# Folding the next batch at the end of the first layer in place of beside the second layer

## The chip, the cores and the metric

The kernel runs on one core of one Trainium2 chip. The metric is device time in microseconds (us) from the first to the last instruction. Engines are named as the profile names them: PE is the matrix engine (PEld its weight loads), DVE the vector engine, ACT the scalar engine, POOL the GpSimd engine and SP the engine whose queue issues most transfers. PSUM is the memory into which PE writes its sums; it is divided into banks, and here each bank tile holds 128 x 512 floats. L927 means line 927 of the kernel's source.

## The reference

There are 8 batches of 576 tokens. An attention with 8 heads gives each token a row of 512 numbers. Then follow a Fourier transform over tokens and columns, of which the real part is added, a normalisation of each row, and two matrix products with a ReLU between them.

```python
q_s = softmax(q, axis=-1); k_s = softmax(k, axis=2)          # cut: written out in full
kv = np.einsum('bhsd,bhse->bhde', k_s, v)                    # one 64x64 matrix per head
x  = np.einsum('bhsd,bhde->bhse', q_s, kv)                   # then heads side by side: (8, 576, 512)
mixed = np.real(np.fft.fft(np.fft.fft(x, axis=1), axis=2))
u  = x + mixed
un = (u - mean(u)) / sqrt(var(u) + 1e-06)
out = u + np.maximum(un @ w_ch1, 0) @ w_ch2                  # 512 -> 2048 -> 512
```

Everything is float32.

## The kernel before

The main loop works on groups of 512 tokens. While PE does the two layers of one group, the vector engines and PE prepare the next batch. For each group `up` is the first layer, `down` is the second. `front(b)` gives two lists of side steps for batch b: `one` is the attention, `two` is the transform and the mixing. The function `merged` spreads a side list evenly over a main list.

```python
def mixed(main, side):
    steps = []
    for i, step in enumerate(main):
        steps.append(step)
        steps += side[i * len(side) // len(main):(i + 1) * len(side) // len(main)]
    return steps
# ... cut
for order, g in enumerate(groups):                # groups 0..6, then 8, then 7
    one, two = front(order + 1, loads) if order + 1 < B else (blk.later, [])
    # ... cut: group 0 has its own, plain form
    jobs, down = blk.up(order, nexts.pop(g)), blk.down(g, order)
    merged(flat(jobs), one)
    merged(down, two + (norm(groups[order + 1]) if order < B else []))
```

From group 1 on, both layers use a Strassen scheme with seven products instead of eight. A first layer is four jobs. Each job runs its products in the order 1, 6, 5, 7, 2, 4, 3 in only three PSUM banks, `ba`, `bb` and `bc`, with one buffer each. Product 7 is added onto product 6 in bank `bb`, so `bb` must have been read (L927) before product 7 may start.

```python
def m1():
    nc.scalar.copy(temp("s1"), box["ba"][:])                                    # L923, ACT
def m6():
    V.tensor_tensor(out=temp("u2"), in0=box["bb"][:], in1=box["s1"][:], op=ALU.add)   # L927, DVE
def m7():
    V.tensor_tensor(out=temp("u3"), in0=box["bb"][:], in1=box["s1"][:], op=ALU.add)   # L931, DVE
    # ... cut
at = {1: "ba", 2: "ba", 6: "bb", 7: "bb", 4: "bb", 5: "bc", 3: "bc"}            # ORDER = (1, 6, 5, 7, 2, 4, 3)
```

In `up` the matmuls are L959. The sums of the last three products go to SBUF on DVE (L970), through the ReLU on ACT (L971), and are then combined on POOL (L363 to L366). In `down` the matmuls are L997; a product is four times as long as in `up`.

The end of the attention of a batch, and the four fold steps with which its transform begins:

```python
def t_times_kv(self, b):                                  # last step of `one`
    # ... PE L672 -> px; ACT copies it to g (L675); PE L678 -> a second px; ACT L679
    V.scalar_tensor_tensor(out=g[:, 1:HD], ...)           # L680, DVE
    V.tensor_tensor(...); V.tensor_tensor(...)            # L682, L683, DVE

def tokens_folded(some=range(4)):                         # two on POOL, two on DVE
    e.tensor_tensor(out=eo[i][:, 0:D], in0=x[i % 2, 0], in1=x[i % 2, 1], op=op)            # L701
def columns_folded(some=range(4)):                        # two on POOL, two on DVE
    e.tensor_tensor(out=t[:, 1:HD], in0=t[:, 1:HD], in1=t[:, D - 1:HD:-1], op=op)          # L707
def by_frequency(some=range(4)):                          # two on POOL, two on DVE
    e.tensor_tensor(out=eo[i][:, NN:], in0=one[:, 0:NN], in1=two[:, 0:NN], op=op)          # L716
def columns_again(some=(2, 3, 0, 1)):                     # eight on DVE
    V.tensor_tensor(out=t[:, 0:QD], in0=y[:, 0:QD], in1=y[:, HD:QD:-1], op=ALU.subtract)   # L722
    V.tensor_tensor(out=y[:, 0:QD], in0=y[:, 0:QD], in1=y[:, HD:QD:-1], op=ALU.add)        # L723
def folded():
    columns_again()
    if b + 1 < B:
        self.keys_from(b + 1, eo[1])                      # loads two keys of the next batch; L496 on DVE
# ... cut
folds = [tokens_folded, columns_folded, by_frequency, folded] if b else [at_first]
return folds + [lambda: None] * (b > 1) + [lambda k=k: block(k) for k in (2, 3, 0, 1, 4)]
```

Each `block` multiplies the folded tiles `eo` by Fourier tables on PE (L754, and L757 with the tile `g`). After the blocks come the mixing steps and the normalisation of the next group.

The framework's scheduler takes the steps in this order as its guide and fixes the final order of instructions on every engine when the kernel is built. Each engine then takes its own list from the top.

Of the kernel before, what the change touches and what calls it, by code (L numbers as in the profile page):

```python
# [47 lines left out]
B, H, S, DH = 8, 8, 576, 64  # L48
# [35 lines left out]
# [9 lines that stand above are left out]
def merged(main, side):  # L93
    for step in mixed(main, side):
        step()
# [959 lines left out]
@with_exitstack  # L1055
def kernel(ctx: ExitStack, tc: tile.TileContext, q, kT, v, w1, w2, ft,
                                                           cd, out):
    blk = _Block(ctx, tc, q, kT, v, w1, w2, ft, cd, out)
    blk.Z = {}

    def front(b, loads=None):

        first = blk.attention(b, loads)
        steps = late(lambda: blk.transform(b), (6, 9, 10)[min(b, 2)])
        mixes = [lambda c=c: blk.mix_own(b, c) for c in range(2)]
        if b % 2:

            mixes.insert(0 if b == B - 1 else 2, lambda: blk.mix_shared(b // 2))
        return first, steps + mixes

    def late(make, n):

        box = []

        def run(i):
            if not box:
                box.extend(make())
            box[i]()

        return [lambda i=i: run(i) for i in range(n)]  # L1080

    nexts = {}

    def norm(g):
        def make():
            nexts[g], steps = blk.norm(g)
            return steps
        return late(make, 7)

    def flat(steps):  # L1090
        return [s for step in steps for s in step]

    fetch, convert = blk.weights()

    after = {}
    for i, place in enumerate(WORDS_AT):
        later = [n for n in range(i + 1, 2 * NF) if WORDS_AT[n] == place]
        if later:
            after[i] = later[0]

    def round_blocks(some):
        for i in some:
            convert(i)
            if i in after:
                fetch(after[i])

    blk.first(fetch)
    free = blk.hold()
    one, two = front(0)
    maxima, some, others = blk.second_keys()  # L1110
    for step in one + [maxima] + some[:1] + two[:1] + some[1:] + others[:1] + two[1:] + others[1:] + norm(0):
        step()

    groups = [*range(B - 1), B, B - 1]
    for order, g in enumerate(groups):
        loads = [] if g == 0 else None
        one, two = front(order + 1, loads) if order + 1 < B else (blk.later, [])
        if g == 0:
            unT = nexts.pop(0)
            up, down = blk.plain(0, unT)  # L1120

            round_blocks(range(1))
            blk.gate(unT[:, 0, 0, :], blk.raws[NF][0:1, 0:2])
            round_blocks(range(1, 4))
            n = 2 * NF - 10
            for f in range(NF):
                up[f]()
                free(f)
                round_blocks(range(4 + n * f // NF, 4 + n * (f + 1) // NF))

            blk.gate(blk.h0[:, NF - 1, :], blk.raws[26][0:1, 0:2])
            turn = (0, 16, 19, 21, 23, 25)
            rest = [lambda i=i: round_blocks([i]) for i in range(4 + n, 2 * NF)]
            combine = [lambda l=l, p=p: blk.combine(l, p) for l in range(2) for p in range(NP)]
            combine[NP:NP] = [lambda i=i: blk.load(15 + i) for i in range(3)]
            combine.append(lambda: blk.load(18))
            for step in loads:
                step()
            for i in LATE_WORDS:
                fetch(i)  # L1140

            blk.spare_words = blk.raws[LATE_WORDS[0]].bitcast(F32)

            side = one + two + norm(1)
            gaps = [6, 3, 6] + [3] * (len(one) - 3) + [3] * 5 + [1] * 4 + [2] * (len(two) - 9) + [1] * 7
            at = 0
            for i in range(len(down)):
                down[i]()
                if i == turn[1]:
                    for n in range(27, 32):  # L1150
                        blk.gate(blk.xpart(1, 0, 0), blk.raws[n][0:1, 0:2])
                if i in turn:
                    rest[turn.index(i)]()
                for step in combine[i * len(combine) // 60:(i + 1) * len(combine) // 60]:
                    step()
                while side and at + gaps[0] <= i:
                    at += gaps.pop(0)
                    side.pop(0)()
            for step in side:
                step()  # L1160
            continue

        jobs, down = blk.up(order, nexts.pop(g)), blk.down(g, order)

        merged(flat(jobs), one)
        merged(down, two + (norm(groups[order + 1]) if order < B else []))

# [51 lines left out]
```

## Time and profile before

| what | value |
|---|---|
| time, median of 3 runs (lowest to highest) | 1127.93 us (1127.23 to 1129.03) |
| span of the profiled run | 1125.2 us |
| PE busy | 1089.7 us, 97% |
| DVE busy | 543.0 us, 48% |
| ACT busy | 403.3 us, 36% |
| POOL busy | 334.1 us, 30% |
| DMA engines, mean share of q1 | 49.9% |

The profile page gives busy times per engine, then the span in 40 slices with the busy share of each engine in tenths. The trace can also be asked for instructions in order of time, where the column after the start is the duration and a bracket names an idle stretch before the instruction and the one that ended it. It can also be asked for the busy time of each engine in chosen stretches. In these PEclk is the share of the full PE clock that was granted. Two layers of one group together take about 121 us in the middle of the kernel, so batch 5, for example, is prepared between 680 and 802 us.

### The profile page before, as it was taken

How to read it: one execution, taken by the hardware profiler on the slowest of the kernel's cores; microseconds unless marked ns; L12 is line 12 of the kernel's file. 1: busy time of each engine (PE TensorE's matmuls, PEld its weight loads, DVE VectorE, ACT ScalarE, POOL GpSimd, SP SyncE). 2: the span in 40 equal slices, each digit the busy share in tenths (PEclk: the TensorE clock that was granted, in tenths of full speed). 3: DMA queues.
4: the chain of work that ended last, by engine and by line, in shares of the span. 5: the costliest groups of instructions: out<-in, count | busy, mean ns of one | idle time of the engine just before them, and what ended most of it. 6: DMA issues, size and time to landing. Idle time of an engine off the chain costs nothing.

```text
span 1125.2 us, 14588 instructions
## 1 busy us (share of the span) xinstructions
PE 1089.7 (97%) x5440; PEld 913.3 (81%) x5440; DVE 543.0 (48%) x1117; ACT 403.3 (36%) x973; POOL 334.1 (30%) x304
## 2 busy tenths in 40 slices
PE   5799999999999999999999999999999999999997
PEld 4644456888888888888889888888889888888886
DVE  6784795378334833484434643683335252103301
ACT  6695424264324413361325232532333152201200
POOL 2064671244022510433123402351035203402320
PEclk9999999999999999999999999999999999999999
DMA  9566685554356434663455436543454444544441
GB/s 310 172 219 196 243 306 197 153 205 169 107 193 202 169 108 145 205 222 112 156 179 184 151 128 194 199 160 113 152 179 150 145 144 141 187 140 157 153 187 56
DMA packets 92581, 193.79 MB, mean 172 GB/s; under 512 B 23120, under 2 KB 59728, under 8 KB 85344
## 3 DMA queue, kind: packets, MB, share of 16 engines
q1 hardware_dynamic: 90712, 191.82, 49.9%
q10 hardware_dynamic: 1800, 1.05, 0.3%
q8 instruction: 43, 0.70, 0.3%
q14 instruction: 26, 0.21, 0.1%
HBM read 168.72 MB, written 28.31 MB: 175 GB/s over the span
## 4 chain that ended last, share of the span: by engine, by line
PE 86%; issue 1%; ACT 1%; DVE 0%; POOL 0%; ACTq 0%; POOLq 0%
PE bb L959 15%; PE bb L997 15%; PE ba L959 10%; PE bc L997 10%; PE bc L959 10%; PE ba L997 10%; PE acc L569 2%; PE acc L657 2%; PE bc L898 2%; PE acc L754 2%; PE acc L757 2%; PE acc L778 1%; PE tr L859 1%; PE tr L624 1%; PE tr L555 1%; PE ba L898 1%
## 5 line engine op out<-in xcount | busy, mean ns | idle before, releaser
L959 PE MATMUL bb<-unT,big 128*128 128x256 f32 x768 | 187.4, 381 | 0.0
L997 PE MATMUL bb<-big 128*128 128x256 f32 x768 | 172.1, 379 | 0.0
L959 PEld LDWEIGHTS bb<-unT,big 128*128 128x128 f32 x768 | 142.8, 190 | 23.6 <-DVE u L927 2.6
L997 PEld LDWEIGHTS bb<-big 128*128 128x128 f32 x768 | 145.4, 190 | 20.3
L363 POOL TENSOR_TENSOR big<-big 128x512 f32<-128x512 f32 (+1 forms) x38 | 46.2, 1217 | 306.9 <-ACT big L971 306.0
L971 ACT ACTIVATE big<-big 128x512 f32<-128x512 f32 x96 | 60.3, 629 | 182.6 <-DVE big L970 182.1
L959 PE MATMUL bc<-unT,big 128*128 128x256 f32 x512 | 125.4, 379 | 0.0
L959 PE MATMUL ba<-unT,big 128*128 128x256 f32 x512 | 123.6, 379 | 0.2 <-ACT unT L863 0.2
L997 PE MATMUL bc<-big 128*128 128x256 f32 x512 | 116.0, 379 | 0.5 <-DVE x L1014 0.5
L997 PE MATMUL ba<-big 128*128 128x256 f32 x512 | 114.8, 379 | 0.0
L931 DVE TENSOR_TENSOR u<-bb,s 128x512 f32<-128x512 f32 x40 | 27.6, 691 | 178.0 <-PE bb L997 120.7
L997 PEld LDWEIGHTS bc<-big 128*128 128x128 f32 x512 | 96.1, 190 | 14.3 <-DVE x L1014 0.9
L997 PEld LDWEIGHTS ba<-big 128*128 128x128 f32 x512 | 95.7, 190 | 12.1
L959 PEld LDWEIGHTS bc<-unT,big 128*128 128x128 f32 x512 | 95.1, 190 | 12.6
L959 PEld LDWEIGHTS ba<-unT,big 128*128 128x128 f32 x512 | 95.1, 190 | 12.2 <-ACT unT L863 0.5
L371 POOL TENSOR_TENSOR unT<-unT 128x512 f32<-128x512 f32 x8 | 14.2, 1774 | 182.5 <-DVE unT L370 182.5
L608 ACT ACTIVATE q<-q,qm 128x64 f32<-128x64 f32 x240 | 61.9, 340 | 6.3 <-DVE qm L606 6.0
L927 DVE TENSOR_TENSOR u<-bb,s 128x512 f32<-128x512 f32 x40 | 27.6, 690 | 72.9 <-PE bb L959 38.7
L970 DVE TENSOR_TENSOR big<-bc,u 128x512 f32<-128x512 f32 x64 | 44.1, 690 | 22.8 <-PE bc L959 21.7
L1009 POOL TENSOR_TENSOR x<-x,u 128x512 f32<-128x512 f32 x14 | 17.7, 1267 | 113.8 <-DVE u L931 101.6
L863 ACT COPY unT<-tr 128x512 f32<-128x512 f32 x36 | 20.8, 586 | 79.9 <-PE tr L859 79.3
L970 DVE TENSOR_TENSOR big<-bb,s 128x512 f32<-128x512 f32 x32 | 22.1, 691 | 56.0 <-PE bb L959 56.0
(256 smaller groups left out, 1647.8 us busy)
## 6 DMA issues: line engine op xcount, KB each, us to landing
big<-w1s SPq DMA_DIRECT2D x64, 896.0 KB
big<-w2s SPq DMA_DIRECT2D x56, 1024.0 KB
big<-in_w_dram SPq DMA_DIRECT2D x21, 512.0 KB
q<-in_q_dram SPq DMA_DIRECT2D x27, 256.0 KB
k<-in_kT_dram SPq DMA_DIRECT2D x24, 288.0 KB
v<-in_v_dram SPq DMA_DIRECT2D x24, 256.0 KB
words<-in_w_dram SPq DMA_DIRECT2D x8, 512.0 KB
mirror<-x SPq DMA_DIRECT2D x14, 256.0 KB
```

The source lines that it names most:

```text
L363: e1.tensor_tensor(out=to(4), in0=at(2), in1=at(3), op=ALU.add)
L569: nc.tensor.matmul(pk, lhsT=ks[:, c, :], rhs=v[:, c, :], start=(c == 0), stop=(c == NC - 1))
L608: nc.scalar.activation(heads[:, h, :], heads[:, h, :], ACT.Exp, bias=m[:, h:h + 1])
L657: nc.tensor.matmul(px[:, r * P:(r + 1) * P], lhsT=qT[:, r, :], rhs=self.kvr[b % 2][:, r, :], start=True, stop=True)
L754: nc.tensor.matmul(full[:, at:at + size], lhsT=t[:, own], rhs=self.ft[:, f + at:f + at + size], start=at == 0, stop=False, skip_group_chec ...
L898: nc.tensor.matmul(po[:], lhsT=h[:, f, i * P:(i + 1) * P], rhs=self.w2sb[:, f, :], start=(f == 0), stop=(f == NF - 1))
L927: V.tensor_tensor(out=temp("u2"), in0=box["bb"][:], in1=box["s1"][:], op=ALU.add)
L931: V.tensor_tensor(out=temp("u3"), in0=box["bb"][:], in1=box["s1"][:], op=ALU.add)
L959: nc.tensor.matmul(bank()[:, i, :], lhsT=w[:, WA_AT[m], k * P:(k + 1) * P], rhs=unT[:, B_AT[m], k, :], start=first and i == 0 and k == 0, ...
L970: V.tensor_tensor(out=hp(i), in0=bank[:], in1=u[:], op=ALU.add)
L971: nc.scalar.activation(hp(i), hp(i), ACT.Relu)
L997: nc.tensor.matmul(bank()[:, i, :], lhsT=h[p][:, A_AT[m], i * P:(i + 1) * P], rhs=w[:, p, :], start=first and i == 0 and p == 0, stop=p == ...
```

## The change

The four fold steps of the transform move from the front of the second layer's side list to the end of the first layer's, for batches 2 to 7. Batch 1 is prepared in the plain form of group 0, and batch 0 ahead of it; both stay as they were.

```diff
         jobs, down = blk.up(order, nexts.pop(g)), blk.down(g, order)
 
+        if order + 1 < B:
+            one, two = one + two[:4], two[4:]
         merged(flat(jobs), one)
         merged(down, two + (norm(groups[order + 1]) if order < B else []))
```

No operation is added or removed. The attention's steps now share the first layer with four more, and the second layer has four fewer, so its blocks, mixing and normalisation are spread over it from an earlier point. The purpose is to have the folded tiles ready when the second layer begins, and to give its side steps more room.

## The prediction

> **What bounds the kernel now.** I read the page first, then the busy time by stage, then the instructions in order of time around one switch from the first to the second layer, on DVE and on PE, and last the one place where PE had stood still for long. The page's slices say that PE is the bound from the third slice on:
>
> ```profile
> PE   5799999999999999999999999999999999999997
> ```
>
> The busy time by stretch sharpens that. The two rows are the first and the second layer while batch 5 is prepared. The first number after the stretch is its length, the second PE's busy time. The sum is over twelve such layers, 317 to 1022 us.
>
> ```profile
> 680.36:744.34 63.98, 63.36 (x353) 56.12 (x353) 37.89 (x71) 29.64 (x77) 20.35 (x17) 1.00 0.56 185
> 744.34:801.57 57.23, 57.23 (x291) 50.73 (x291) 27.83 (x62) 14.68 (x36) 14.32 (x12) 1.00 0.41 147
> ...
> sum 704.50, PE 703.26 PEld 622.99 DVE 317.68 ACT 230.87 POOL 193.98; mean PE 58.60 PEld 51.92 DVE 26.47 ACT 19.24 POOL 16.16
> ```
>
> PE is idle for 704.50 - 703.26 = 1.2 us of it. A change that removes no matmul can win almost nothing here; it can only lose. Next, DVE at the switch (start, duration):
>
> ```profile
> 743.93 0.68 DVE L970 TENSOR_TENSOR big<-bc,u 128x512 f32<-128x512 f32 x1
> 745.79 1.12 DVE L680 SCALAR_TENSOR_TENSOR eo<-eo,sign 128x255 f32<-128x255 f32 x1 [1.17 <-ACT eo L675]
> 746.83 1.75 DVE L701 TENSOR_TENSOR eo<-x 128x512 f32<-128x512 f32 x1
> 748.51 1.35 DVE L682 TENSOR_TENSOR eo<-eo 128x128 f32<-128x128 f32 x1
> 749.78 1.75 DVE L701 TENSOR_TENSOR eo<-x 128x512 f32<-128x512 f32 x1
> 751.46 0.81 DVE L683 TENSOR_TENSOR eo<-eo 128x128 f32<-128x128 f32 x1
> 752.19 2.35 DVE L707 TENSOR_TENSOR eo<-eo 128x255 f32<-128x255 f32 x2
> 754.57 1.70 DVE L716 TENSOR_TENSOR eo<-eo 128x257 f32<-128x257 f32 x2
> ...
> 761.02 0.69 DVE L927 TENSOR_TENSOR u<-bb,s 128x512 f32<-128x512 f32 x1
> ```
>
> The first fold cannot start before L680, which waits for L675, the copy of the attention's last product. From L680 to the end of L707 takes 754.54 - 745.79 = 8.75 us, and L716 adds 1.7. All of it lies after the last L970 of the first layer, so no bank of that layer waits for it. On PE the same time looks like this:
>
> ```profile
> 743.28 1.06 PE L678 MATMUL acc<-kvr,tq 128*128 128x128 f32 x8
> 744.17 7.07 PE L997 MATMUL ba<-big 128*128 128x256 f32 x32
> 751.08 7.07 PE L997 MATMUL bb<-big 128*128 128x256 f32 x32
> 757.99 0.66 PE L754 MATMUL acc<-ft,eo 128*128 128x144 f32 x4
> ```
>
> A matmul starts every (751.08 - 744.17) / 32 = 0.216 us. The two products between L678 and the first block (L754) cover 13.8 us, and the folds just fit beneath them. That cover is what the change touches. Lastly the long idle stretch, and the clock in the 2 us stretches that follow it (third number from the end):
>
> ```profile
> 142.79 1.34 PE L657 MATMUL acc<-kvr,qT 128*128 128x128 f32 x8 [4.15 <-ACT qT L631]
> ```
>
> ```profile
> 142.00:144.00 2.00, 1.21 (x9) 1.21 (x10) 2.00 (x3) 2.00 (x5) 1.92 (x2) 0.91 0.21 81
> 144.00:146.00 2.00, 2.00 (x7) 1.45 (x6) 2.00 (x3) 1.97 (x4) 1.30 (x2) 0.50 0.04 14
> 146.00:148.00 2.00, 2.00 (x4) 0.71 (x3) 2.00 (x4) 0.00 (x0) 1.10 (x2) 0.74 1.00 393
> ```
>
> After 4.15 us of idleness PE ran slow: 2 x (0.09 + 0.50 + 0.26) = 1.7 us of clock were lost on top of the wait.
>
> [...] The trace agrees: its order at the switches is that of the built program. So the built order of the changed kernel tells who stands behind whom. [...] L701 on DVE takes 0.67 us at the least and 1.75 us in the median, because POOL works at the same time, while L927 with one PSUM input takes 0.69 always. [...]
>
> **The change, part by part.** Removed and added: nothing; PE's 0.216 us steps stay the same in number. Moved: the folds. Let T be the end of L678 on PE. L680 starts at about T + 0.3: L672 ends 0.9 before T, the copy L675 takes 0.57, and in the old trace L680 of batch 3 starts at 380.18, with L678 ended at 379.80. The folds cannot start earlier than in the old kernel, since L680 still stands ahead of them in DVE's list. What moves is PE's work around them. In the built order of the changed kernel I find four forms.
>
> *Batch 2.* L678 still ends the first layer, but now only one product of the second layer, 16 source matmuls or 32 steps, stands before the first block. PE reaches L754 at T + 32 x 0.216 = T + 6.9. Block 2 needs the second L723 on the DVE tiles. In the old trace of batch 3 that is 10.0 us after L680 (380.18 to 390.18), so at T + 10.3. Stall 3.4 us.
>
> *Batches 3 and 5.* The attention now ends before the whole last job of the first layer. PE does products 1, 6 and 5, each 8 x 0.216 = 1.73 us, and wants product 7 at T + 5.2. That needs L927, and on DVE L927 stands behind L680, L701, L682, L701, L683, L707 twice, L722, L716 twice, L723 and L722. Working: 0.2 + 8.4 (between the 8.1 of batch 3 and the 8.75 above) + 1.8 (L716 at 0.7 to 1.7 for two, three small ones at 0.2 each) gives L927 at T + 10.4, ended at T + 11.1. Stall 5.9, and L931 behind eight more small ones and two key maxima (L543, 1.35 for two) makes product 4 wait another 0.5. Together 6.4 us each.
>
> *Batches 4 and 6.* L678 lies in the middle of the last job's first product, so product 7 is wanted at T + 0.86 + 3.46 = T + 4.3. L927 stands behind one L722 of a POOL tile, and POOL has L363 to L366 of the third job (1.3 to 1.6 each), two L701, two L707 and an L716 ahead of it. From about T - 1, after the L971 that releases L363, that is 4 x 1.45 + 2 x 1.55 + 2 x 0.95 + 0.8 = 11.6, so L722 at T + 10.6 and L927 ended at T + 11.5. Stall about 7.0 us each.
>
> *Batch 7.* As for 3 and 5, with L716 twice and one L722 before L927: T + 0.3 + 8.75 + 1.7 + 0.25 + 0.69 = T + 11.7 against T + 5.2. Stall 6.5 us.
>
> Sum of waits: 3.4 + 2 x 6.4 + 2 x 7.0 + 6.5 = 36.7 us, all on PE, which has no slack to take it up. Clock: each of the five long stalls exceeds the 4.15 us that cost 1.7; an estimate with three in four of them[...] is 5 x 1.7 x 0.75 = 6.4 us. On the other side at most the 1.2 us of idleness can come back. Sum: 1127.9 + 36.7 + 6.4 - 1 = 1170 us.
>
> **The rivals.** *Nothing happens (1127 to 1132 us):* DVE is busy 48% and could hide the folds anywhere. For it speaks that busy share; against it the built order, in which L927 cannot pass the folds. *Only the clash of DVE and POOL matters:* were POOL idle during the folds, L701 would take 0.67, L680 0.47, and the chain to L707 about 3.5 us; L927 would end near T + 6 and the stalls would be 1 us each, 1135 us in all. Against it speaks POOL's list, which in every form holds sums of the last but one job (L363 to L366) and its own folds at that time. *It gains (1120 to 1126):* the second layer gets room and each next first layer starts sooner. Against it: PE is busy for the whole of 744.34 to 801.57, so there is no wait to remove. *A denser first layer stalls also before its last job (1175 to 1190):* DVE runs nearly without gaps from 720 to 744 us already, and the attention is now squeezed into some three quarters of the steps. Of this I can't size anything.
>
> **Range and chances.** If the stalls are two thirds of what I worked out and the clock mostly holds, the time is 1128 + 24 + 1 = 1153; with the full sum, every clock loss and a denser first layer it is about 1186. I take 1150 to 1186 as the range. The limit for slower by 2% is 1150.5. Chances: 0.01 faster, 0.12 within 2%, 0.87 slower.
>
> **What would show it right or wrong.** Right: in the preparation of batches 3 to 7 PE stands idle once for 5 to 7 us before a product 7 in `bb`, released by L927; for batch 2 before an L754, released by DVE; and the granted clock dips after these. The first layers of batches 3 to 7 grow from 62.6 to 64.1 us to about 69 or 70, while the second layers keep their length or shrink by the side steps they lost. Wrong, if L680 or the folds start well before T, if DVE's L701 falls to 0.7 us, or if the lost time lies in transfers. The forms' single sizes may be off by 2 us each[...].

## The result, and the profile after

The changed kernel takes 1189.72 us (1187.94 to 1190.33) against 1128.47. The ratio is 1.0537, with a 95% interval of 1.0522 to 1.0553. That is 61 us more, where I had predicted 42 more. The direction was right, the size lies above my range.

The page's slices answer to those shown of the kernel before. Each digit is the busy share of one fortieth of the span, and of the granted clock in the second row:

```profile
PE   5799899898999899979999899979997999999997
PEclk9999999898999899989999999989999999999999
```

PE now has holes at regular distances, and its clock falls near many of them. The busy time by stretch says in which layer. These are the first and the second layer of group 5, the same two that the prediction showed of before. Groups are counted from 0 and group 5 works beside batch 6, so the stretch from 680 to 802 us prepares batch 6 and not, as said there, batch 5:

```profile
723.50:798.00 74.50, 65.77 (x353) 57.06 (x352) 43.57 (x90) 30.27 (x77) 25.29 (x22) 0.95 0.46 155
798.00:855.20 57.20, 57.20 (x291) 50.68 (x290) 17.43 (x42) 14.39 (x38) 9.38 (x8) 1.00 0.43 151
```

The first layer grew from 64 to 74.5 us. The second is as long as before (57.2), although it lost the fold steps: PE was its bound, so freeing DVE there gave nothing back. In the first layer PE's idle time grew from 0.6 to 8.7 us (74.50 - 65.77), and its busy time from 63.4 to 65.8 us for the same matmuls; its mean clock there is 0.95.

What PE waited for between 195 and 980 us (total, times, longest):

```profile
PE bb L959 <- DVE u L927: 31.1, 5, 7.8
PE tr L555 <- ACT k L545: 5.4, 8, 2.3
PE acc L754 <- DVE eo L723: 4.8, 1, 4.8
PE tr L624 <- issue: 2.1, 1, 2.1
```

Three smaller rows, 1.7 us together, are left out here. In the kernel before, this is the whole list for the same times:

```profile
PE acc L569 <- ACT ks L556: 1.9, 3, 0.6
PE ba L959 <- ACT unT L863: 0.2, 1, 0.2
```

None of PE's waits in either list was ended by a transfer. The first row of the changed kernel holds the five waits of product 7 behind the folds, the third the wait of the first block beside batch 2. Both are in the prediction's sum. The second and fourth are not. Now the end of the first layer of group 5 in order of time, on DVE, on POOL and on PE:

```profile
777.31 0.68 DVE L680 SCALAR_TENSOR_TENSOR eo<-eo,sign 128x255 f32<-128x255 f32 x1 [0.73 <-ACT eo L675]
778.02 1.24 DVE L682 TENSOR_TENSOR eo<-eo 128x128 f32<-128x128 f32 x1
779.18 1.75 DVE L701 TENSOR_TENSOR eo<-x 128x512 f32<-128x512 f32 x1
...
783.80 2.34 DVE L707 TENSOR_TENSOR eo<-eo 128x255 f32<-128x255 f32 x2
788.24 0.29 DVE L722 TENSOR_TENSOR eo<-eo 128x128 f32<-128x128 f32 x1 [2.10 <-POOL eo L716]
788.45 0.68 DVE L927 TENSOR_TENSOR u<-bb,s 128x512 f32<-128x512 f32 x1
789.05 0.76 DVE L716 TENSOR_TENSOR eo<-eo 128x257 f32<-128x257 f32 x2
```

```profile
776.41 1.29 POOL L363 TENSOR_TENSOR big<-big 128x512 f32<-128x512 f32 x1 [14.52 <-ACT big L971]
...
783.29 1.70 POOL L366 TENSOR_TENSOR big<-big 128x512 f32<-128x512 f32 x1
784.96 1.76 POOL L707 TENSOR_TENSOR eo<-eo 128x255 f32<-128x255 f32 x2
786.80 1.41 POOL L716 TENSOR_TENSOR eo<-eo 128x257 f32<-128x257 f32 x2
```

```profile
776.34 1.06 PE L678 MATMUL acc<-kvr,tq 128*128 128x128 f32 x8
...
779.83 1.89 PE L959 MATMUL bc<-unT,big 128*128 128x256 f32 x8
789.19 3.78 PE L959 MATMUL bb<-unT,big 128*128 128x256 f32 x8 [7.47 <-DVE u L927]
```

L927 needs 0.68 us, but in DVE's list it stands behind L680, the folds L701 and L707 and one L722; the two L716 of DVE come after it. That L722 works on a tile of POOL's, so POOL's list has to come down to L716 first. L927 starts 11.2 us after L678 has ended (777.23, where PE's next matmuls start). PE wanted `bb` at about 781.6. When it goes on, eight matmuls take 3.78 us in place of 1.89. The granted clock, third number from the end, was about half in that time:

```profile
785.00:787.00 2.00, 0.00 (x0) 0.00 (x0) 1.14 (x2) 0.00 (x0) 1.92 (x3) 0.77 0.00 0
787.00:789.00 2.00, 0.00 (x0) 0.00 (x0) 0.76 (x2) 0.00 (x0) 1.21 (x2) 0.50 0.00 0
789.00:791.00 2.00, 1.81 (x4) 1.52 (x5) 2.00 (x10) 0.00 (x0) 0.00 (x0) 0.50 0.02 4
791.00:793.00 2.00, 2.00 (x6) 1.59 (x5) 0.87 (x4) 0.00 (x0) 0.00 (x0) 0.53 0.00 0
```

While PE was busy again it lost 1.81 x 0.50 + 2.00 x 0.47 = 1.85 us. Worked out in the same way, the six long waits are followed by 2.9, 2.2, 2.0, 1.5, 1.9 and 2.5 us of lost clock, 13 us in all.

### The profile page after: what moved, and what is told of

It reads as the page before. It is cut to its first block, busy times and chain, and to the rows that moved or that the text cites. A ratio compares the mean times of both kernels' runs of the same rounds, so it can differ in the third digit from the quotient of the medians.

```text
span 1188.0 us, 14574 instructions
## 1 busy us (share of the span) xinstructions
PE 1108.6 (93%) x5440; PEld 923.7 (78%) x5440; DVE 532.8 (45%) x1117; ACT 405.4 (34%) x973; POOL 335.3 (28%) x304
## 4 chain that ended last, share of the span: by engine, by line
PE 77%; DVE 7%; POOL 3%; issue 3%; ACT 2%; DMA 1%; SPq 0%; ACTq 0%; POOLq 0%; DVEq 0%
PE bb L997 14%; PE bb L959 13%; PE bc L997 9%; PE ba L997 9%; PE ba L959 8%; PE bc L959 8%; PE acc L569 2%; PE bc L898 2%; PE acc L657 2%; PE acc L754 2%; PE acc L757 1%; PE acc L778 1%; PE tr L859 1%; PE tr L555 1%; PE tr L624 1%
## 5 line engine op out<-in xcount | busy, mean ns | idle before, releaser
L959 PE MATMUL bb<-unT,big 128*128 128x256 f32 x768 | 195.7, 394 | 31.1 <-DVE u L927 31.1
L959 PEld LDWEIGHTS bb<-unT,big 128*128 128x128 f32 x768 | 149.4, 198 | 55.1 <-DVE u L927 34.2
L997 PE MATMUL bb<-big 128*128 128x256 f32 x768 | 176.0, 382 | 0.0
L363 POOL TENSOR_TENSOR big<-big 128x512 f32<-128x512 f32 (+1 forms) x38 | 47.7, 1256 | 315.7 <-ACT big L971 314.8
L959 PE MATMUL ba<-unT,big 128*128 128x256 f32 x512 | 126.1, 384 | 0.2 <-ACT unT L863 0.2
L959 PE MATMUL bc<-unT,big 128*128 128x256 f32 x512 | 125.4, 379 | 0.0
L959 PEld LDWEIGHTS ba<-unT,big 128*128 128x128 f32 x512 | 97.5, 194 | 13.4 <-ACT unT L863 0.5
L959 PEld LDWEIGHTS bc<-unT,big 128*128 128x128 f32 x512 | 95.1, 190 | 11.8
L927 DVE TENSOR_TENSOR u<-bb,s 128x512 f32<-128x512 f32 x40 | 27.6, 690 | 149.5 <-PE bb L997 98.0
L923 ACT COPY s<-ba 128x512 f32<-128x512 f32 x40 | 23.4, 584 | 100.5 <-PE ba L959 62.8
L970 DVE TENSOR_TENSOR big<-bc,u 128x512 f32<-128x512 f32 x64 | 44.1, 689 | 26.7 <-PE bc L959 25.9
```

The lines of the kernel that those rows point to most:

```text
L363: e1.tensor_tensor(out=to(4), in0=at(2), in1=at(3), op=ALU.add)
L959: nc.tensor.matmul(bank()[:, i, :], lhsT=w[:, WA_AT[m], k * P:(k + 1) * P], rhs=unT[:, B_AT[m], k, :], start=first and i == 0 and k == 0, ...
L970: V.tensor_tensor(out=hp(i), in0=bank[:], in1=u[:], op=ALU.add)
L997: nc.tensor.matmul(bank()[:, i, :], lhsT=h[p][:, A_AT[m], i * P:(i + 1) * P], rhs=w[:, p, :], start=first and i == 0 and p == 0, stop=p == ...
```

## The experiments

The theory after the traces: DVE takes its list from the top (product 6 of the last job stood in `bb` at 779.99, and L927 began at 788.45, once its turn came), the scheduler puts folds ahead of the last job's L927 as soon as the attention ends before that job, and PE's idleness then costs clock as well (1.5 to 2.9 us after each long wait). Rivals: the cost comes from where the fold steps stand, whatever the attention does; or from a denser attention alone; or from something that goes with an early fold (transfers, POOL at work at the same time). All edits are shown against the changed kernel; where nothing else is said, they hold for batches 2 to 7.

**1. Batch 2 as before.**

```diff
-        if order + 1 < B:
+        if 1 < order and order + 1 < B:
```

> The change for batches 3 to 7 alone; batch 2 is prepared as before. In the traces the two layers beside batch 2 take 139.3 us after the change and 121.8 before, so if the cost of each batch stays where it arises, this run takes 1189.7 - 17.5 = 1172 us. If batch 2 cost what I had predicted for it (3.4 us, and the rest came from a shift carried on to later layers), 1186 us.

Measured 1172.5 us, ratio 1.0386 (1.0371 to 1.0402). The cost of each batch stays where it arises, and batch 2 alone costs 17 us, by far the most. I had given it 3.4.

**2. The fold steps stay in the second layer, only the attention ends early.**

```diff
-            one, two = one + two[:4], two[4:]
+            one = one + [lambda: None] * 4
```

> The fold steps stay at the front of the second layer; four empty steps stand at the end of the attention's list, so that the attention ends as early as in the changed kernel. Theory: it is the early end of the attention that hurts, because the scheduler then puts L680 and the folds ahead of the last job's L927 on DVE in any case; five of the six long waits stay, only the one of batch 2 before its first block (4.8 us and about 2.9 us of clock) goes: 1182 us. Rival: the place of the fold steps is what hurts: about 1128 us, or up to 1140 if the denser attention has waits of its own.

Measured 1183.63 us, ratio 1.0485 (1.0469 to 1.0501). Here not one fold step was moved, and nine tenths of the cost are there. In the built order folds stand ahead of L927 all the same; it seems that the scheduler takes them up as soon as L680 stands in front of them. The end of the first layer of group 5 on DVE is that of the changed kernel, operation by operation:

```profile
776.93 2.34 DVE L707 TENSOR_TENSOR eo<-eo 128x255 f32<-128x255 f32 x2
781.37 0.29 DVE L722 TENSOR_TENSOR eo<-eo 128x128 f32<-128x128 f32 x1 [2.10 <-POOL eo L716]
781.58 0.68 DVE L927 TENSOR_TENSOR u<-bb,s 128x512 f32<-128x512 f32 x1
```

The rival that blames the place of the fold steps falls for all but the last tenth. What hurts is the attention's last step before the last job, or the denser attention by itself; experiment 5 separates the two.

**3. The attention with its old spacing, the folds between the layers, the blocks early.**

```diff
-        if order + 1 < B:
-            one, two = one + two[:4], two[4:]
+        folds, two = (two[:4], two[4:]) if order + 1 < B else ([], two)
         merged(flat(jobs), one)
+        for step in folds:
+            step()
```

> The attention keeps its old spacing, the four fold steps run between the layers, and the blocks are spread over the second layer as in the changed kernel. Then L927 is free of the folds, but PE meets the first block after one product (6.9 us) in place of two (13.8 us). From the old trace the last fold that a first block needs ends 10.4 to 13.3 us after L678, so the waits are 3.5 to 6.4 us, 32 us over six batches, and with 2.3 us of clock for each of them 1128 + 32 + 14 = 1174 us. Rival: only the wait behind L927 matters: 1128 to 1132 us.

Measured 1170.62 us, ratio 1.0369 (1.0343 to 1.0396). L927 is free, and PE waits at the first block, in all six batches. Its waits:

```profile
PE acc L754 <- DVE eo L723: 31.0, 6, 6.5
```

The sum of 32 us came from the old trace and holds to 1 us; the clock and whatever else came on top was 11 us (41.7 - 31.0) in place of the 14 expected. So the second way of paying for the change is that the blocks come one product earlier while the folds do not. In the changed kernel it is met beside batch 2 alone.

**4. The same with the blocks one product later.**

```diff
-        folds, two = (two[:4], two[4:]) if order + 1 < B else ([], two)
+        folds, two = (two[:4], [lambda: None] * 4 + two[4:]) if order + 1 < B else ([], two)
```

> As the run before, with four empty steps ahead of the blocks, so that the blocks come after two products again. Theory: nothing is left of the cost, since neither L927 nor a block waits for a fold: 1128 us, plus or minus 2. Rival: something else that goes with folding at that time (transfers of the next keys, the turns of DVE and POOL) costs: over 1135 us.

(The edit is against the third experiment.) Measured 1128.77 us, ratio 1.0000 (0.9991 to 1.0008). Calling the folds between the layers costs nothing and wins nothing. The trace says why: beside batch 6 the order on DVE from L680 on is that of the kernel before, and the first block follows 12.2 us after L680 in both (748.13 to 760.34, and 745.79 to 757.99). So the place of the fold steps in the source doesn't matter as long as the same order comes out of it. What a fold at another time would meet in transfers or in POOL's work isn't tested by this run.

**5. The squeezing alone.** The attention is as dense as in the changed kernel, but its last step and the folds come after the last job.

```diff
-            one, two = one + two[:4], two[4:]
+            one, end = one[:-1] + [lambda: None] * 5, one[-1:]   # end = [] before
         merged(flat(jobs), one)
+        for step in end:
+            step()
```

> The attention is squeezed as in the changed kernel, but its last step (the products L672 and L678 with L680) and the folds stay where they were, after the last job. This leaves the squeezing alone. In the changed kernel's trace the first layer beside batch 2 has 6 us of small waits and about 3.4 us of slow clock that the old one has not, and those beside batches 4 and 6 about 1 us each: 1128 + 12 = 1140 us. Rival: squeezing costs nothing by itself: 1128 to 1131 us.

Measured 1144.81 us, ratio 1.0150 (1.0130 to 1.0169). It is a cost of its own, 16.3 us (the interval is 14.7 to 19.1), a little more than expected. PE's waits in it, of which the kernel before has none:

```profile
PE tr L555 <- ACT k L545: 5.4, 8, 2.3
PE bb L959 <- DVE u L931: 2.9, 2, 1.5
PE tr L624 <- issue: 2.1, 1, 2.1
```

How it arises shows best beside batch 2, where the changed kernel has the same wait of 2.34 us as this run. First the kernel before, then the changed kernel, each on PE and on DVE:

```profile
223.01 1.03 PE L959 MATMUL ba<-unT,big 128*128 128x256 f32 x4
223.87 1.03 PE L959 MATMUL bb<-unT,big 128*128 128x256 f32 x4
224.74 1.03 PE L959 MATMUL bc<-unT,big 128*128 128x256 f32 x4
225.60 0.60 PE L555 MATMUL tr<-ident,k 128*128 128x128 f32 x4
```

```profile
223.21 0.69 DVE L970 TENSOR_TENSOR big<-bc,u 128x512 f32<-128x512 f32 x1 [1.03 <-PE bc L959]
223.82 0.74 DVE L543 TENSOR_REDUCE km<-k 128x1 f32<-128x576 f32 x1
```

```profile
222.03 1.89 PE L959 MATMUL bc<-unT,big 128*128 128x256 f32 x8
226.26 1.12 PE L555 MATMUL tr<-ident,k 128*128 128x128 f32 x4 [2.34 <-ACT k L545]
```

```profile
223.96 0.69 DVE L970 TENSOR_TENSOR big<-bc,u 128x512 f32<-128x512 f32 x1 [1.03 <-PE bc L959]
224.56 0.74 DVE L543 TENSOR_REDUCE km<-k 128x1 f32<-128x576 f32 x1
```

The key's maximum L543 stands in both behind the L970 of the `bc` product that PE has just done. Before, three half products of the next job covered L970, L543 and L545; with the denser list the key's transpose stands directly behind the product, and PE waits. A second wait (2.1 us, which the profile calls issue) comes before the transpose of a query tile. In the changed kernel the L618 that normalises a query tile ends at 255.3, and that transpose starts at 255.42, so L618 is the likely releaser; the profile names none.

One part stays open. DVE waits for query tiles that are still being loaded (before L606) for 5.4 us between 195 and 980 us in the kernel before, 14.8 us here and 15.3 in the changed kernel. None of PE's waits was ended by a transfer, but what late queries add to the waits further down was not separated.

**6. Useless matmuls in two of the waits.** 9 beside batch 2 and 12 beside batch 7.

```diff
             one, two = one + two[:4], two[4:]
+            if order == 1:
+                two[0] = lambda: blk.warm(blk.ft[:, 0:HD], 9)      # two[0] was the empty step
...
             parts = product(m, lambda m=m: box[at[m]], first, m in (2, 4, 3))
+            if m == 7 and filler:                                  # 12 in the last job beside batch 7
+                parts.insert(0, lambda: self.warm(self.ft[:, 0:HD], filler))
```

> The changed kernel with useless matmuls on PE where it waits: 9 (3.9 us) in the wait of batch 2 before its first block, and 12 (5.2 us) in that of batch 7 before product 7. Both are shorter than the waits (4.8 and 6.3 us), and DVE's order there stays the same. If the slow matmuls after a wait come from the clock, which is cut by idleness, the work added makes the kernel faster: the trace shows 2.9 and 2.1 us lost after these two waits, so 1189.7 - 5 = 1184.7 us, with a granted clock of 1.00 there. If they are slow for another reason, 1189.7 us or more.

Measured 1184.71 us, ratio 1.0501 (1.0487 to 1.0516). More work on PE made the kernel 5 us faster. Beside batch 7 (L206 are the added ones; the added source lines make L961 of what is L959 elsewhere):

```profile
906.80 5.34 PE L206 MATMUL tr<-ft,ident 128*128 128x256 f32 x24
913.25 1.99 PE L961 MATMUL bb<-unT,big 128*128 128x256 f32 x8 [1.11 <-DVE u L927]
```

```profile
914.00:916.00 2.00, 2.00 (x11) 1.76 (x10) 1.39 (x4) 0.00 (x0) 0.00 (x0) 1.00 0.00 0
```

Product 7 now runs at its full pace (1.99 in place of 3.78 us), at a clock of 1.00. Beside batch 2 the first block starts at 279.83, and the clock stays at 1.00 there too:

```profile
280.00:282.00 2.00, 2.00 (x12) 1.76 (x12) 2.00 (x8) 0.21 (x1) 0.00 (x0) 1.00 0.78 295
```

The 5.0 us won come close to what the clock had cost after these two waits, 2.9 and 2.5 us by the working above (the text before the run put the second at 2.1). So the slow matmuls after them are the clock's, and the clock's fall is idleness's.

**7. POOL without its sums.** L363 to L366 are left out in groups 2 to 6, so the second layer there multiplies stale numbers; the time is read for what DVE and POOL do to each other.

```diff
-                    if i == 2:
+                    if i == 2 and at not in range(2, 7):
                         self.a_side(hp, hp, nc.gpsimd, nc.gpsimd)
```

> The changed kernel without POOL's sums L363 to L366 in groups 2 to 6 (beside batches 3 to 7), so the second layer there multiplies stale numbers; PE's work is the same. POOL then has only its own folds at the end of the first layer. If the clash of DVE and POOL makes the folds long (8.8 us from L680 to the last L707, of which some 3.5 us would be left), the five waits before product 7 shrink from 31 us to about 5 us and most of their clock loss goes: about 1154 us. If the folds are as long without it, 1190 us.

Measured 1155.25 us, ratio 1.0234 (1.0220 to 1.0248). PE's waits for L927 are nearly gone:

```profile
PE bb L959 <- DVE u L927: 4.7, 4, 1.9
```

Beside batch 3 the order on DVE is that of the changed kernel. There L927 now starts 5.2 us after L680 (385.81 to 390.98) in place of 9.5 (385.87 to 395.32), and PE's wait is 0.48 us in place of 4.76. The same L722 takes 0.27 us in place of 1.35. First this run, then the changed kernel:

```profile
389.70 0.27 DVE L722 TENSOR_TENSOR eo<-eo 128x128 f32<-128x128 f32 x1
390.98 0.67 DVE L927 TENSOR_TENSOR u<-bb,s 128x512 f32<-128x512 f32 x1
```

```profile
392.97 1.35 DVE L722 TENSOR_TENSOR eo<-eo 128x128 f32<-128x128 f32 x1
395.32 0.68 DVE L927 TENSOR_TENSOR u<-bb,s 128x512 f32<-128x512 f32 x1
```

So beside batch 3 the folds' place in the list makes the wait, and POOL's sums, which run at the same time, make nine tenths of its length. Over all five waits it is 31 us with the sums and 5 without. But for batches 4, 6 and 7 the order on DVE shifted a little with the edit, and for 4 and 6 the sums also stood in POOL's list ahead of the L716 that DVE waited for, so there these parts aren't separated.

**8. The squeezing alone, with batch 2 at its old spacing.** The edit is against the fifth experiment.

```diff
-        if order + 1 < B:
+        if 1 < order and order + 1 < B:
             one, end = one[:-1] + [lambda: None] * 5, one[-1:]
```

> As the run that squeezes the attention alone (1144.8 us), but batch 2 keeps its old spacing. In that run's trace the two layers beside batch 2 take 131.2 us against 121.8 in the old kernel, and the other five pairs together 7 us more than before. If the cost of the squeezing lies with batch 2 for the greater part, this run takes 1144.8 - 9.4 = 1135.4 us. If all batches share it evenly (2.7 us each): 1142 us.

Measured 1136.01 us, ratio 1.0066 (1.0052 to 1.0080). Of the 16.3 us of squeezing, 8.8 lie beside batch 2.

**9. The opposite of the change.** The attention's last step moves to the front of the second layer.

```diff
-            one, two = one + two[:4], two[4:]
+            one, two = one[:-1], one[-1:] + two
```

> The opposite of the change: the last step of the attention moves from the first layer to the front of the second, and the folds stay behind it; the rest of the attention has more room in the first layer. Theory: PE is the bound and has some 3 us of waits left after 195 us, so at most that can be won: 1125 to 1128 us. Rival: the folds now end later than the two products that cover them (12.1 us after L678 in place of 13.8), and the first blocks wait: 1130 to 1145 us.

Measured 1135.82 us, ratio 1.0067 (1.0053 to 1.0080). The rival of this run holds: PE waits at the first blocks again (4.1 us in five waits, released by L723), the largest part of the 7.4 us lost. So of the three places tried for the last step, that of the kernel before is the best. No run here is faster than that one.

## Why the prediction was right and wrong

Two runs and the two kernels make a sum. From 1128.5 us, squeezing the attention gives 1144.8 (experiment 5), letting its last step come before the last job 1183.6 (experiment 2), and moving the blocks forward, which only beside batch 2 still makes a wait, 1189.7 (the change). The parts are 16.3, 38.8 and 6.1 us, good to 2 or 3 us each, an estimate from the spread of the runs (1142.9 to 1148.5 us in experiment 5).

- *The wait of product 7 behind the folds.* Right. Predicted for batches 3 to 7 were 6.4, 7.0, 6.4, 7.0 and 6.5 us, measured 4.8, 7.8, 4.8, 7.5 and 6.3. The way through POOL's list for batches 4 and 6 was seen as it is (2.10 us of waiting for L716). Batches 3 and 5 came out shorter by 1.6: the first L701 started just before POOL's sums did and took 0.68 us in place of 1.75, and the further 0.5 us before product 4 did not come at all.
- *The wait of batch 2 before its first block.* Predicted 3.4, measured 4.8: L680 started 1.5 us after the end of L678 and not 0.3, because DVE was still busy with query tiles (L606 to L618, until 271.5).
- *The clock.* Mis-sized: 6.4 predicted, 13 measured after the six long waits. I took 1.7 us for each, from the one wait of 4.15 us in the kernel before, and only three in four to be hit, and none for batch 2. The three in four was my assumption; no trace had shown it. All six were hit, with 1.5 to 2.9 each.
- *The step that failed* is the term that the sum left out: the fourth rival, a first layer so dense that it stalls before its last job as well. I wrote "Of this I can't size anything" and put it into the sum of 1170 at nothing. Squeezing alone costs 16.3 us (experiment 5), 8.8 of them beside batch 2 (experiment 8). The changed kernel's own trace gives about 14 us for it: the span grew by 62.8 us (1125.2 to 1188.0), and the six long waits take 35.9 of that, the clock after them 13. The built order already showed it: beside batch 2 the key's transpose had lost the three half products in front of it.
- *What was missing, by size.* The sum lacks 21 of those 62.8 us: 14 are the term left out and 6 the clock. The upper end of the range, 1186, did allow for "every clock loss and a denser first layer": 1127.9 + 36.7 + 5 x 1.7 - 1 leaves 14 us for the latter. What carried the time beyond that end was therefore the clock, at 13 us in place of 8.5.
- *The other rivals.* That nothing would happen, or that the kernel would gain, fell as argued. The clash of DVE and POOL goes far to decide the size of the waits: without POOL's sums the five came to 4.7 us (experiment 7), about the 1 us each that this rival gave. But it is not away in the changed kernel, so that rival's 1135 us was not to be had.
- *Where the cost would show.* In the first layers, as said; for batches 3 to 7 they were predicted at 69 to 70 us and take 69 to 75. The second layers did not change their length, except beside batch 2, where the early block waits.

## What to carry to other kernels

When one engine is busy all the time, look at what covers each wait before moving side work: here the same folds cost nothing behind the last job and 39 us in front of it, and spreading a list over fewer steps took the cover from waits that had nothing to do with the folds. Read the built order of every engine, not only the order of the steps in the source, and size each wait that has lost its cover, the small ones too. A vector instruction of 0.7 us that frees a bank should not stand behind eight to twelve that free none, as L927 did here.

## What was not expected of the hardware

The one fall that I knew from the kernel before came after 4.15 us of idleness. Here the clock also fell after shorter waits, and not after every one. In the changed kernel a wait of 2.34 us (from 223.9), with a second one of 0.52 at 227.6, was followed by a clock of 0.50 from 228 to 232. Without POOL's sums a wait of 1.87 us (until 764.22) was followed by this:

```profile
764.00:766.00 2.00, 1.78 (x7) 1.58 (x8) 2.00 (x9) 0.00 (x0) 0.00 (x0) 0.90 0.02 4
766.00:768.00 2.00, 2.00 (x6) 1.58 (x5) 2.00 (x8) 0.59 (x1) 0.00 (x0) 0.50 0.00 0
```

In the same run a wait of 1.92 us beside batch 4 (until 517.39) was followed by a clock of 1.00 throughout. In experiment 3, of two waits of 3.46 and 3.44 us (until 400.77 and 656.09), the first was followed by a dip (0.50 from 402 to 404) and the second by none (1.00 until 664). So waits of almost the same length came with a dip and without one, at 1.9 us as at 3.4, and the length of a wait alone does not tell which. What else decides it was not tried.
